# A 128-byte padding tile ahead of the probability, weight, K and V tiles of a cached GQA attention block

## The chip, the cores and the metric

The kernel runs on one core of a Trainium2 chip. The metric is the device time of one execution in microseconds. Before the change the median of 12 runs is 192.56 us (192.39 to 192.72).

## The reference

A block of grouped-query attention for decoding: 8 sequences with 4 new tokens each, 32 query heads on 8 key/value heads, a cache of 2048 positions, head size 128, all in bfloat16.

```python
q = (x @ wq).reshape(B, Sq, Hq, Dh).transpose(0, 2, 1, 3)      # x: (8, 4, 512), wq: (512, 4096)
k = repeat(k_cache, 4, axis=1)                                  # k_cache, v_cache: (8, 8, 2048, 128)
v = repeat(v_cache, 4, axis=1)
p = softmax(q @ k^T * 128 ** -0.5)
return (p @ v).transpose(0, 2, 1, 3).reshape(B, Sq, 4096) @ wo  # wo: (4096, 512)
```

K and V are 33.6 MB each, wq and wo 4.2 MB each: some 75.5 MB are read once, and little else moves.

## The kernel before

**Units.** The work is cut into 32 units `(p, b)`: a pair `p` of key/value heads of one sequence `b`. A unit's K is one tile `k_sb` of 128 partitions by 32 x 128 elements (8 KB in each partition, 1 MB in all); partition `s` holds 32 neighbouring cache positions, so each partition is filled from one unbroken run of 8 KB in HBM. V is laid out in the same way in `v_sb`. `kpool` has 7 buffers and `vpool` has 6.

**Loads.** All loads are issued by SyncE (SP), in the order of the list `loads` that is made at L113 to L121: `wq` (L111, 32 KB in each partition) and `x` (L112) first, then K three units ahead of V in turn, and the pieces of `wo` (L109) behind the last of them. `load_ready` (L123) issues what has a free buffer; it is called once in each half-unit step. `wo_sb` takes over the place of `wq_sb` in SBUF (L189; the pool `wpool` has one buffer). `wo` comes in two pieces of 8 KB in each partition, three of 4 KB and two of 2 KB.

**Steps.** The loop at L317 goes over half units. Each step transposes half of a K tile on TensorE through PSUM (L199; two bf16 values travel as one fp32), copies the result to `kt` (L206 on VectorE, a quarter of them at L204 on ScalarE), forms the scores of the half before (L217) and their exponentials into `probs` (L227), sums the probabilities with a matrix of ones (L255, L263, L267), multiplies them with V (L241) and scales (L272). After each head pair the result is transposed (L284, L299), and at the end it is multiplied with `wo` (L309), evacuated (L361, L362) and stored (L363, L364). The order on each engine is the order of the code (`manual_schedule`, L65).

**Placement in SBUF.** The pools are laid out one behind the other in the order of L53 to L58, and the tiles of `const` in the order in which the code names them. An address below is the byte at which a tile starts in each partition. `const` begins with `x_sb` at 16,512, which is 32 x 512 + 128; with the sizes of the tiles that follow, `xT_sb` (256 bytes) being the first that is no multiple of 512, `qT_all` and all that come behind it up to `ident` start 384 bytes past a multiple of 512, `ones` 128 bytes past one, and `probs` again 384. Since `probs`, `wq_sb`/`wo_sb`, `k_sb`, `v_sb` and `kt` are whole multiples of 512 bytes, each of their buffers starts 384 bytes past a multiple of 512, that is, 128 past a multiple of 256: `wq_sb` and `wo_sb` at 44,928, the first `k_sb` at 77,696, the first `v_sb` at 135,040, the first `kt` at 184,192.

Of the kernel before, what the change touches and what calls it, by code (L numbers as in the profile page):

```python
# [8 lines left out]
BF16 = mybir.dt.bfloat16  # L9
# [5 lines left out]
def kernel(  # L15
# [37 lines left out]
    const = ctx.enter_context(tc.tile_pool(name="const", bufs=1))  # L53
# [24 lines left out]
    oP = [const.tile([128, WR, T], BF16, name=f"oP{p}") for p in range(G2)]  # L78
    ident = const.tile([128, 128], BF16, name="ident")
    ones = const.tile([128, 128], BF16, name="ones")  # L80
    probs = [const.tile([128, C, NQ], BF16, name=f"probs{i}") for i in range(L // 2 + 2)]

    units = [(p, b) for p in range(G2) for b in range(B)]
# [311 lines left out]
```

The softmax here doesn't subtract the row's maximum and nothing guards it: scores larger than these inputs give would overflow.

## Time and profile before

| | |
|---|---|
| median of 12 runs | 192.56 us (192.39 to 192.72) |
| the profiled execution, time of the run | 192.41 us |
| its span, first to last instruction | 190.6 us |
| granted TensorE clock | 1.0 |
| busy: PE, PE weight load, VectorE, ScalarE | 152.7, 139.5, 113.8, 86.2 us |
| read from HBM | 75.53 MB, 396 GB/s over the span |
| K and V load: size, median from issue to landing | 1024 KB, 19.9 us |
| longest wait of TensorE for DMA within the loop | 10.8 us in all, for K (L199) |

The span leaves out what lies ahead of the first instruction and behind the last: 1.8 us of the run. Busy times of different engines overlap, so they don't add up to the span. TensorE is busy for 80% of it, but the row of the DMA engines (shown below) is the one that is full from the start to the last load.

### The profile page before, as it was taken

What the parts mean: (1) busy time and instruction counts of PE and PEld (TensorE: products, weight loads), DVE (VectorE), ACT (ScalarE), POOL (GpSimd) and SP (SyncE); (2) the same over time, 40 slices, a digit from 0 to 9 for tenths busy, and PEclk for the clock granted to TensorE, in tenths of its full rate; (3) what the DMA queues carried; (4) which work ended last, traced back from release to release, by engine and by line L of the source; (5) the groups of instructions that cost most, each with busy time, mean ns of one, the idle gap of its engine ahead of it and who ended that gap; (6) DMA issues with size and microseconds to landing.
All of it is one profiled execution on the core that took longest, in us unless ns stands there. A gap on an engine that the chain in (4) does not pass through costs nothing.

```text
span 190.6 us, 6429 instructions
## 1 busy us (share of the span) xinstructions
PE 152.7 (80%) x2861; PEld 139.5 (73%) x2892; DVE 113.8 (60%) x220; ACT 86.2 (45%) x170; POOL 1.1 (1%) x8
## 2 busy tenths in 40 slices
PE   0019887899999999978888889998885899998683
PEld 0018776799989998867888878887774788886572
DVE  6411745577767777666666667776663677672420
ACT  2003466665566654555544444454553555551000
POOL 2000000000000000000000000000000000000000
PEclk9999999999999999999999999999999999999999
DMA  6999999999999999999999999999999999999950
GB/s 227 433 407 421 419 425 411 425 419 421 418 414 416 428 411 416 425 418 419 421 416 423 418 416 423 414 418 423 418 421 416 418 428 413 416 424 414 413 206 9
DMA packets 10539, 75.97 MB, mean 399 GB/s; under 512 B 1200, under 2 KB 1296, under 8 KB 1936
## 3 DMA queue, kind: packets, MB, share of 16 engines
q1 hardware_dynamic: 10464, 75.55, 95.8%
q8 instruction: 22, 0.36, 0.8%
q14 instruction: 5, 0.04, 0.1%
q10 hardware_dynamic: 48, 0.02, 0.0%
HBM read 75.53 MB, written 0.03 MB: 396 GB/s over the span
## 4 chain that ended last, share of the span: by engine, by line
DMA 90%; PE 7%; DVE 1%; ACT 0%; issue 0%; SPq 0%
DMA k_sb<-in_k_cache_dram 74%; DMA wo_sb<-in_wo_dram 9%; DMA x_sb<-in_x_dram 6%; PE psq L161 2%; PE out_ps L309 2%; PE kp L199 2%; DVE q_bd L185 1%; PE pse L176 1%; ACT q_bd L185 0%; PE xtp L152 0%; PE s_ps L217 0%; SPq L111 0%; ACT out_sb L362 0%; DVE xT_sb L155 0%
## 5 line engine op out<-in xcount | busy, mean ns | idle before, releaser
L199 PE MATMUL kp<-ident,k_sb 128*128 128x128 f32 x512 | 80.9, 284 | 10.8 <-DMA k_sb<-in_k_cache_dram 10.8
L206 DVE COPY kt<-kp 128x1024 bf16<-128x1024 bf16 x96 | 65.5, 685 | 27.0 <-PE kp L199 26.4
L227 ACT ACTIVATE probs<-s_ps 64x256 bf16<-64x256 f32 x128 | 48.3, 378 | 69.0 <-PE s_ps L217 68.2
L199 PEld LDWEIGHTS kp<-ident,k_sb 128*128 128x128 f32 x512 | 55.2, 143 | 12.2 <-issue 11.8
L217 PE MATMUL s_ps<-q_bd,kt 128*128 128x64 bf16 x1024 | 42.1, 193 | 3.1 <-ACT kt L204 2.6
L217 PEld LDWEIGHTS <-kt 128*128 128x128 bf16 x1024 | 39.6, 98 | 4.8 <-ACT kt L204 3.1
L241 PEld LDWEIGHTS <-v_sb 128*128 128x128 bf16 x1024 | 34.2, 96 | 9.7 <-DMA v_sb<-in_v_cache_dram 2.5
L263 DVE TENSOR_REDUCE l_sb<-l_ps 128x32 f32<-128x512 f32 x32 | 22.1, 692 | 24.0 <-PE l_ps L255 21.2
L241 PE MATMUL o_ps<-probs,v_sb 128*128 128x32 bf16 x1024 | 35.0, 176 | 1.3 <-DMA v_sb<-in_v_cache_dram 1.2
L204 ACT COPY kt<-kp 128x1024 bf16<-128x1024 bf16 x32 | 32.4, 1012 | 0.8
L255 PE MATMUL l_ps<-probs,ones 128*128 128x512 bf16 x33 | 12.4, 380 | 1.5
L267 DVE RECIPROCAL r_sb<-l_sb 128x32 f32<-128x32 f32 x32 | 11.3, 353 | 1.1
L152 PE MATMUL xtp<-ident,x_sb 32*128 32x32 bf16 x4 | 0.5, 190 | 13.5 <-DMA x_sb<-in_x_dram 13.3
L152 PEld LDWEIGHTS <-x_sb 32*128 32x128 bf16 x4 | 0.3, 115 | 13.6 <-DMA x_sb<-in_x_dram 13.3
L309 PE MATMUL out_ps<-wo_sb,oP 128*32 128x256 bf16 x64 | 7.6, 272 | 1.3 <-DMA wo_sb<-in_wo_dram 1.3
L168 ACT ACTIVATE qT_all<-psq 128x256 bf16<-128x256 f32 x4 | 1.5, 383 | 14.6 <-PE psq L161 14.6
L309 PEld LDWEIGHTS <-oP 128*32 128x32 bf16 x64 | 6.1, 96 | 2.0 <-issue 1.2
L362 ACT CAST out_sb<-out_ps 32x256 bf16<-32x256 f32 x1 | 0.4, 361 | 15.1 <-PE out_ps L309 15.1
L272 DVE TENSOR_TENSOR oT_all<-o_ps,r_sb 128x32 bf16<-128x32 f32 x32 | 5.8, 182 | 1.7 <-PE o_ps L241 1.5
L255 PEld LDWEIGHTS <-ones 128*128 128x128 bf16 x64 | 6.0, 98 | 0.8 <-issue 0.4
L185 DVE CAST q_bd<-pse 64x512 bf16<-64x512 f32 x4 | 2.6, 683 | 4.7 <-PE pse L176 4.7
L155 DVE COPY xT_sb<-xtp 128x32 bf16<-128x32 bf16 x4 | 0.5, 170 | 6.8 <-PE xtp L152 6.8
(23 smaller groups left out, 34.4 us busy)
## 6 DMA issues: line engine op xcount, KB each, us to landing
k_sb<-in_k_cache_dram SPq DMA_DIRECT2D x32, 1024.0 KB, 19.9
v_sb<-in_v_cache_dram SPq DMA_DIRECT2D x32, 1024.0 KB, 19.9
wq_sb<-in_wq_dram SPq DMA_DIRECT2D x1, 4096.0 KB, 12.3
wo_sb<-in_wo_dram SPq DMA_DIRECT2D x2, 1024.0 KB, 18.7
wo_sb<-in_wo_dram SPq DMA_DIRECT2D x3, 512.0 KB, 17.5
wo_sb<-in_wo_dram SPq DMA_DIRECT2D x2, 256.0 KB, 13.4
x_sb<-in_x_dram SPq DMA_DIRECT2D x1, 32.0 KB, 12.1
out_dram<-out_sb SPq DMA_DIRECT2D x1, 16.0 KB, 1.4
```

The costliest lines, as they stand in the source:

```text
L185: (nc.scalar.copy if g else nc.vector.tensor_copy)(out=q_bd[rows, p, :, :, g, :], in_=pse[rows, :, :, :])
L199: nc.tensor.transpose(kp[:, j, :], k4[:, w : w + 128], ident4[:, :])
L204: nc.scalar.copy(out=kt2, in_=kp2)
L206: nc.vector.tensor_copy(out=kt2, in_=kp2)
L217: nc.tensor.matmul(s_ps[:, 2 * j : 2 * j + 2, :], lhsT=k_t[:, j % (HC // 4), :, e], rhs=q_bd[:, p, e, b, :, :], start=(e == 0), stop=(e == 1),
L227: nc.scalar.activation(out=pr[rows, hf * HC : (hf + 1) * HC, cols], in_=s_ps[rows, :, cols], func=EXP)
L241: nc.tensor.matmul(o_ps[u][:, :], lhsT=vs[u][:, cc, :], rhs=pr[:, cc, :], start=(cc == 0), stop=(cc == C - 1),)
L255: nc.tensor.matmul(l_ps[:, :, :], lhsT=ones[:, :], rhs=pr[:, c : c + LC, :], start=(c == 0), stop=(c + LC == C),)
L263: nc.vector.tensor_reduce(out=l_sb[:, :], in_=l_ps[:, :, :].rearrange("d c q -> d q c"), axis=AX, op=ADD)
L267: nc.vector.reciprocal(r_sb[:, :], l_sb[:, :])
L272: nc.vector.tensor_tensor(out=oT_all[:, p * HP : (p + 1) * HP, b, :], in0=o_ps[u][:, :].rearrange("d (h s) -> d h s", h=HP), in1=r_sbs[u][ ...
L309: nc.tensor.matmul(out_ps[half][:, :], lhsT=oP[p][:, r, :], rhs=wo_sb[:, p, r, half * DH : (half + 1) * DH], start=(p == 0 and r == 0), st ...
```

## The change

One tile more is named in the pool `const`, between `ones` and `probs`. Nothing reads or writes it.

```diff
     ident = const.tile([128, 128], BF16, name="ident")
     ones = const.tile([128, 128], BF16, name="ones")
+    pad = const.tile([128, 64], BF16, name="pad")
     probs = [const.tile([128, C, NQ], BF16, name=f"probs{i}") for i in range(L // 2 + 2)]
```

The tile takes 64 bf16 elements, 128 bytes, in each partition. All that lies behind it moves up by 128 bytes; all ahead of it stays.

| tile | start before | start after | after, past a multiple of 512 |
|---|---|---|---|
| `x_sb` | 16,512 | 16,512 | 128 |
| `q_bd` | 19,840 | 19,840 | 384 |
| `ident4`, `oT_all`, `out_sb`, `oP`, `ident` | | unmoved | 384 |
| `ones` | 34,432 | 34,432 | 128 |
| `probs0` (five of 2,048 bytes) | 34,688 | 34,816 | 0 |
| `wq_sb`, `wo_sb` | 44,928 | 45,056 | 0 |
| `k_sb`, first of 7 (8,192 bytes each) | 77,696 | 77,824 | 0 |
| `v_sb`, first of 6 (8,192 bytes each) | 135,040 | 135,168 | 0 |
| `kt`, first of 6 (2,048 bytes each) | 184,192 | 184,320 | 0 |
| `l_sb` (two of 128 bytes) | 196,480 | 196,608 | 0 and 128 |
| `r_sb` (two of 128 bytes) | 196,736 | 196,864 | 256 and 384 |
| `nat_sb`, first of 2 | 196,992 | 197,120 | 0 |

PSUM is laid out as before. The instructions of every engine, their order and their waits are the same in both programs; only the addresses in SBUF differ.

## The prediction, as it was written before the changed kernel ran

> **What bounds the kernel now.** I read the page's DMA rows first, then the chain that ended last, then the waits of SP's queue, then the busy times by stretch. In the DMA rows each digit is the busy share of the 16 DMA engines in one fortieth of the span (9 is 90% or more), GB/s is what they moved, and q1 is the queue that carries all of SP's loads.
>
> ```profile
> DMA  6999999999999999999999999999999999999950
> GB/s 227 433 407 421 419 425 411 425 419 421 418 414 416 428 411 416 425 418 419 421 416 423 418 416 423 414 418 423 418 421 416 418 428 413 416 424 414 413 206 9
> DMA packets 10539, 75.97 MB, mean 399 GB/s; under 512 B 1200, under 2 KB 1296, under 8 KB 1936
> ...
> q1 hardware_dynamic: 10464, 75.55, 95.8%
> ```
>
> The engines are full from the second slice to the last load. Only the length of each packet, or the number of bytes, can shorten that. The chain in order of time (start, duration, what) says the same.
>
> ```profile
> 1.17 12.05 DMA x_sb<-in_x_dram
> ...
> 20.80 2.56 PE kp L199 x12
> 23.36 0.50 PE s_ps L217 x16
> 23.85 0.63 PE kp L199 x6
> 24.48 19.80 DMA k_sb<-in_k_cache_dram
> ...
> 166.48 17.48 DMA wo_sb<-in_wo_dram
> ...
> 184.00 3.67 PE out_ps L309 x32
> ```
>
> From 24.48 to 184.00 us it is loads only. Each step is one load from issue to landing; it takes 19.80 us because seven others are queued ahead of it: 8 x 1.0486 MB in 19.80 us is 423.7 GB/s. The waits of SP's queue (total us, times, longest) show what lets the next load go.
>
> ```profile
> SPq L102 <- DMA v_sb<-in_v_cache_dram: 56.0, 25, 3.6
> SPq L92 <- DMA k_sb<-in_k_cache_dram: 50.7, 25, 2.1
> ...
> SPq L102 <- PE o_ps L241: 4.4, 4, 2.2
> ```
>
> Nearly always it is an earlier landing. TensorE held a load back a few times, for 2.2 us at most, while some 7 loads of about 2.5 us each were still queued: the stream doesn't run dry.
>
> **The change.** It removes no instruction, adds none, moves none on any engine and adds no wait. It shifts SBUF addresses by 128 bytes: loads of wq, wo, K and V write from a multiple of 512 instead of 384 past one; TensorE, VectorE and ScalarE meet probs, kt and V at other addresses.
>
> *DMA packets, the one item on the path.* How many: 64 K and V loads of 128 rows are 8192 packets of 8 KB; wo is 256 of 8 KB, 384 of 4 KB, 256 of 2 KB; wq is 128 of 32 KB. That is 9216, or 576 for each of the 16 engines. (The rest of q1 are 4-byte completions and the few rows of x and out, which stay where they were.)
>
> How long one takes: q1's 95.8% of 16 x 190.6 us is 2921.5 us of packet time. The trace's packet records give the commonest duration by size: 1 KB 46 ns, 2 KB 84, 4 KB 159, 8 KB 309, 32 KB 1213. The slope from 4 to 32 KB is (1213 - 159) / 28,672 = 0.03676 ns a byte, 27.2 GB/s for an engine; what is left is 8.4 ns for each packet (159 - 150.6), the same for 1 KB and for 32 KB. The mean 8 KB packet is 314.6 ns, 5.5 over its commonest: jitter.
>
> So 8.4 ns a packet and the jitter are all that an address could touch. Bounds: nothing (the 8.4 ns belong to any packet), or all of the 8.4 ns: 576 x 8.4 = 4.8 us. With the jitter gone too it would be 576 x 13.9 = 8.0 us, and I see no reason for that. Below nothing: see the last rival.
>
> [...] And every large packet of this trace with an SBUF end starts 128 past a multiple of 256, x and out included, so no row shows an aligned one. [...]
>
> *Where the 2.7 us land.* Head: x lands at 13.22 us behind wq's 8 packets per engine, 0.04 us sooner. From there to 24.48 us TensorE's chain rules, but seven loads stay queued, so the engines don't stop and the stream gains all the while. End: the last V lands near 180.3 us, with about 560 of the 576 packets of each engine behind it, so 2.6 us sooner; the last wo pieces gain the rest. Behind 184.00 us 3.67 us of L309, the evacuation and the store of 16 KB stand as they were.
>
> *Is TensorE able to follow?* Columns: the stretch, its length, then busy us (count) of PE, weight load, VectorE, ScalarE, POOL, the granted clock, DMA share and GB/s.
>
> ```profile
> 44.00:64.00 20.00, 19.74 (x394) 18.58 (x396) 14.79 (x29) 12.61 (x25) 0.00 (x0) 1.00 1.01 418
> ...
> 84.00:105.00 21.00, 17.14 (x341) 15.83 (x343) 13.46 (x25) 10.86 (x22) 0.00 (x0) 1.00 1.02 421
> ...
> 145.00:166.00 21.00, 17.48 (x337) 16.40 (x342) 13.07 (x26) 9.37 (x21) 0.00 (x0) 1.00 1.01 419
> ```
>
> At 44 to 64 us it is full, catching up from its late start on a stock of loaded tiles; from 84 us on it idles 17 to 18%, waiting for K. The stream gets 1.4% quicker (2.7 of 184 us), so cover remains. If it were gone, the gain would end where TensorE is full: 20 us at 1.4%, 0.3 us given up.
>
> *Operands at new addresses.* L217 (193 ns), L241 (176), L206 (685), L227 (378), L255 (380): no row shows any of them at another address. Bounds: plus or minus a few per cent. PE's 152.7 us lie within 13.3 to 187.7 us, with 21.7 us idle, so a slowdown is hidden until its 2861 matmuls lose some 7 ns each, 4% of L241's duration; a speed-up is worth nothing but a little of the 3.67 us at the end. I take zero.
>
> **Sum.** Against the profiled run: 192.41 - 2.7 = 189.7. That run lies 0.15 under the median, so 192.56 - 2.7 = 189.9 us.
>
> **Rivals.**
> *No effect, 192.6 us.* The 8.4 ns are the packet's own. [...] Chance 0.24.
> [...] Chance 0.12, within "faster".
> *Slower, 195.7 us.* Rows that now all start on the same 512-byte grid meet more often, and the jitter doubles: 5.5 ns x 576 = 3.2 us. For it: mean and commonest packet do differ, so something already collides, and the stream has no slack at all; it decides from 0.7 ns a packet (0.2% of 309). Against it: all buffers already start at one common offset, and their spacing is unchanged. Chance 0.17, most of it for a loss smaller than this.
>
> **Numbers.** 0.2%, 0.4 us, is about what a measurement of this kernel can tell from no change. Forecast (4 cycles, or a gain of that order between 0.4 and 4 us) 0.47; full transaction 0.12; no effect 0.24; slower 0.17. So faster 0.59, same 0.24, slower 0.17. The likeliest alone runs from 188.6 to 192.1. For eight in ten I go from 187.4, near the full transaction, to 192.9, which takes in no effect and a trace of loss.
>
> **What would show it.** Right: the commonest 8 KB packet near 304 to 305 ns, 4 KB near 154, q1's share of packet time down by 2.7 us per engine, slices near 426 GB/s, chain steps of a K load near 19.5 us instead of 19.80, x still at 46 ns and the completions at 9. Matmul durations the same. Wrong: the same packet times with the time unchanged (no effect), a wider gap between mean and commonest packet (the last rival), or quicker packets with SP's queue now waiting for L241 and L199 (TensorE became the bound).

## The result and the profile after

The changed kernel takes 190.18 us (median of 7 runs, 190.07 to 190.37) against 192.57 us for the kernel before (29 runs): the ratio is 0.9878, with a 95% interval of 0.9869 to 0.9887, or 2.4 us. Its profiled execution took 190.18 us with a span of 188.4 us, 2.2 us under the span before. Two of the five executions of dma_on_grid, its profiled one among them, and one of the four of pieces_on_grid took over 1.5% longer than the fastest of their kernel and are left out of the times below.

The DMA rows of the page after:

```profile
DMA  6999999999999999999999999999999999999950
GB/s 223 445 397 426 421 433 417 426 428 421 421 426 421 430 419 423 428 424 419 431 421 421 431 421 423 428 421 426 424 421 430 419 430 423 424 422 418 421 218 9
...
q1 hardware_dynamic: 10464, 75.55, 95.7%
```

There are as many packets and bytes on q1 as before, and the engines are as full as before. But 95.7% of a span of 188.4 us is 180.3 us for each engine, where 95.8% of 190.6 was 182.6 us. So 2.3 us of packet time are gone from each engine, and they are the whole gain.

The chain of waits of the kernel after, in order of time:

```profile
24.31 19.47 DMA k_sb<-in_k_cache_dram
43.80 19.80 DMA k_sb<-in_k_cache_dram
63.62 20.90 DMA k_sb<-in_k_cache_dram
84.53 19.49 DMA k_sb<-in_k_cache_dram
...
144.81 19.50 DMA k_sb<-in_k_cache_dram
164.33 17.42 DMA wo_sb<-in_wo_dram
...
181.80 3.67 PE out_ps L310 x32
```

Of the chain before, the steps behind the first (24.48, 19.80):

```profile
44.30 19.90 DMA k_sb<-in_k_cache_dram
64.22 21.33 DMA k_sb<-in_k_cache_dram
85.57 19.83 DMA k_sb<-in_k_cache_dram
```

The loads still make the chain. The first step is 19.47 us instead of 19.80, the first three together 60.17 instead of 61.03; the last load is through at 181.75 us (164.33 + 17.42), where it was 183.96; the 3.67 us of products behind it are what they were (all lines of the code have moved down by one: L310 is the former L309).

Did TensorE become a bound? First the waits of SP's queue after the change, then the busy times by stretch:

```profile
SPq L103 <- DMA v_sb<-in_v_cache_dram: 55.5, 25, 3.5
SPq L93 <- DMA k_sb<-in_k_cache_dram: 51.2, 26, 2.2
...
SPq L103 <- PE o_ps L242: 2.6, 3, 1.6
```

```profile
44.00:64.00 20.00, 19.79 (x405) 18.82 (x407) 15.35 (x30) 12.08 (x24) 0.00 (x0) 1.00 1.01 423
...
84.00:105.00 21.00, 17.42 (x341) 16.24 (x346) 13.33 (x26) 10.19 (x21) 0.00 (x0) 1.00 1.01 426
...
145.00:166.00 21.00, 20.00 (x361) 18.86 (x366) 13.87 (x27) 10.09 (x20) 0.00 (x0) 0.92 1.01 424
```

It did not: the loads are let go by landings, TensorE holds them back for 2.6 us where it was 4.4, and its share of 84 to 105 us has risen only from 17.14 to 17.42 us. From 145 to 166 us it has risen from 17.48 to 20.00 us, in an execution whose granted clock was 0.92 there instead of 1.00; the chain's step in that stretch (19.50 us) is no longer than the others, so that cost nothing, but little idle time was left. The operands at new addresses cost what they cost before, as the groups of the page after show (busy us, mean ns; before 685, 378, 193 and 176 ns):

```profile
L207 DVE COPY kt<-kp 128x1024 bf16<-128x1024 bf16 x96 | 65.2, 683 | 26.2 <-PE kp L200 25.7
L228 ACT ACTIVATE probs<-s_ps 64x256 bf16<-64x256 f32 x128 | 48.3, 378 | 67.6 <-PE s_ps L218 66.9
...
L218 PE MATMUL s_ps<-q_bd,kt 128*128 128x64 bf16 x1024 | 42.8, 194 | 3.4 <-ACT kt L205 2.6
...
L242 PE MATMUL o_ps<-probs,v_sb 128*128 128x32 bf16 x1024 | 35.1, 177 | 1.0 <-DMA v_sb<-in_v_cache_dram 0.9
```

**What changed within a packet.** The packet records of q1 in the two traces:

| packets of q1 | before: commonest, share of it, mean | after: commonest, share of it, mean |
|---|---|---|
| 8 KB, 8448 | 309 ns, 37%, 314.5 | 309 ns, 99.6%, 310.5 |
| 4 KB, 384 | 159 ns, 62%, 161.0 | 159 ns, 100%, 159.0 |
| 2 KB, 256 | 84 ns, 93%, 84.2 | 84 ns, 100%, 84.0 |
| 32 KB (wq), 128 | 1213 ns, 66%, 1304.8 | 1213 ns, 63%, 1301.7 |
| 4 bytes (completions), 1184 | 9 ns, 84%, 9.5 | 9 ns, 99.7%, 9.0 |

Between these two kernels the commonest duration has not moved for any size. What is gone is the scatter above it. For an engine that is 528 packets of 8 KB by 3.95 ns (2.09 us), 24 of 4 KB by 2.0 (0.05), 74 completions by 0.5 (0.04) and 8 of 32 KB by 3.1 (0.03), in all 2.2 us: the difference of the two spans.

### The profile page after: what moved, and what is told of

Same layout as the page of the kernel before. It is cut to its first block, busy times and chain, and to the rows that moved or that the text cites. A ratio compares the mean times of both kernels' runs of the same rounds, so it can differ in the third digit from the quotient of the medians.

```text
span 188.4 us, 6429 instructions
## 1 busy us (share of the span) xinstructions
PE 152.5 (81%) x2861; PEld 139.3 (74%) x2892; DVE 113.3 (60%) x220; ACT 86.2 (46%) x170; POOL 1.1 (1%) x8
## 3 DMA queue, kind: packets, MB, share of 16 engines
q1 hardware_dynamic: 10464, 75.55, 95.7%
## 4 chain that ended last, share of the span: by engine, by line
DMA 95%; PE 2%; SPq 1%; issue 0%; ACT 0%
DMA k_sb<-in_k_cache_dram 85%; DMA wo_sb<-in_wo_dram 9%; PE out_ps L310 2%; SPq L93 1%; SPq L113 0%; SPq L112 0%; ACT out_sb L363 0%
## 5 line engine op out<-in xcount | busy, mean ns | idle before, releaser
L218 PE MATMUL s_ps<-q_bd,kt 128*128 128x64 bf16 x1024 | 42.8, 194 | 3.4 <-ACT kt L205 2.6
L310 PE MATMUL out_ps<-wo_sb,oP 128*32 128x256 bf16 x64 | 7.6, 272 | 1.0 <-DMA wo_sb<-in_wo_dram 1.0
L310 PEld LDWEIGHTS <-oP 128*32 128x32 bf16 x64 | 6.1, 96 | 1.8 <-issue 1.0
L363 ACT CAST out_sb<-out_ps 32x256 bf16<-32x256 f32 x1 | 0.4, 361 | 14.5 <-PE out_ps L310 14.5
```

Source lines behind the costliest of these rows:

```text
L218: nc.tensor.matmul(s_ps[:, 2 * j : 2 * j + 2, :], lhsT=k_t[:, j % (HC // 4), :, e], rhs=q_bd[:, p, e, b, :, :], start=(e == 0), stop=(e == 1),
L310: nc.tensor.matmul(out_ps[half][:, :], lhsT=oP[p][:, r, :], rhs=wo_sb[:, p, r, half * DH : (half + 1) * DH], start=(p == 0 and r == 0), st ...
```

## The experiments

The question left by these tables is whose scatter it was: that of the written addresses or of the compute engines' operands, of one border or another, of the DMA engines alone or of their meeting with the compute engines. The theories go by letters: A, a write off the border is drawn out where it meets the compute engines in SBUF; B, by itself; C, it is the place of the operands of the compute engines that counts; D and E, two prices that the author set for B (D, the same for any start off the border, at either end and for a packet of any size; E, one that grows with the distance from the border below); F, it is the difference between the read and the written end.

### Which tiles, and which border

Two kernels put only one kind of tile on the border, by gaps of chosen sizes between the pools; three more change the size of the pad.

```diff
 # dma_on_grid: 128 bytes ahead of wpool, 384 bytes ahead of ktpool
+    gap1 = ctx.enter_context(tc.tile_pool(name="gap1", bufs=1))
     wpool = ctx.enter_context(tc.tile_pool(name="wpool", bufs=1))
...
+    gap2 = ctx.enter_context(tc.tile_pool(name="gap2", bufs=1))
     ktpool = ctx.enter_context(tc.tile_pool(name="ktpool", bufs=6))
...
+    gap1.tile([128, 64], BF16, name="pad1")
+    gap2.tile([128, 192], BF16, name="pad2")
```

> Only wq, wo, K and V, the tiles that DMAs write, start on multiples of 512 bytes; probs, kt and the small tiles start 384 past one, as before. Theory A and B (the written end of the DMA packets matters): the whole gain is here, 190.2 us within 0.4, nearly all 8 KB packets at 309 ns. Theory C (what matters is where the tiles lie that TensorE, VectorE and ScalarE read and write in the loop): 192.6 us, two in three packets above 309 ns, mean near 314.6.

```diff
 # engines_on_grid: 128 bytes ahead of probs, 384 ahead of wpool, 128 ahead of ktpool
+    pad = const.tile([128, 64], BF16, name="pad")
...
+    gap1.tile([128, 192], BF16, name="pad1")
+    gap2.tile([128, 64], BF16, name="pad2")
```

> The reverse: probs, kt and the small tiles as in the changed kernel, on multiples of 512; wq, wo, K and V start 384 past one, as before. Theory A and B: 192.6 us within 0.4, mean 8 KB packet near 314.6 ns. Theory C: 190.2 us, packets at 309 ns.

```diff
 # pad_to_256, pad_to_64 and pad_to_32: only the size of the pad
-    pad = const.tile([128, 64], BF16, name="pad")
+    pad = const.tile([128, 192], BF16, name="pad")   # pad_to_256
+    pad = const.tile([128, 32], BF16, name="pad")    # pad_to_64
+    pad = const.tile([128, 80], BF16, name="pad")    # pad_to_32
```

> The pad takes 384 bytes in each partition instead of 128: the same tiles start 256 past a multiple of 512. If the border that matters is one of 256 bytes, as the prediction had it: 190.2 us, packets at 309 ns. If it is one of 512: 192.6 us, packets as before.

> The pad takes 64 bytes: the same tiles start 448 past a multiple of 512, 64 short of a border. If the cost comes with any start off the border: 192.6 us, commonest packet 309 ns and mean near 314.6 as before. If only a start of 128 past one is dear (or if 64 bytes are the grid): 190.2 us. If the distance decides (192 bytes past a 256-byte border instead of 128): between 193 and 195 us.

> The pad takes 160 bytes: the tiles start 32 past a multiple of 512. [...]

Measured, with the packet records of each one's profile (mean of those under 360 ns, which leaves out the few longer ones that come with instruction fetches, 27 in the kernel before):

| kernel | K, V, wq, wo past a 256-byte border | probs, kt past it | us, median | ratio to before, 95% | 8 KB packets at 309 ns, mean in ns |
|---|---|---|---|---|---|
| before | 128 | 128 | 192.57 | | 37%, 312.9 |
| changed | 0 | 0 | 190.18 | 0.9869 to 0.9887 | 99.6%, 309.0 |
| dma_on_grid | 0 | 128 | 190.24 | 0.987 to 0.991 | 99.5%, 309.0 (from 60 us on) |
| engines_on_grid | 128 | 0 | 192.57 | 0.9993 to 1.0011 | 36%, 312.9 |
| pad_to_256 | 0 (256 past one of 512) | 0 | 190.15 | 0.9862 to 0.9891 | 99.5%, 309.0 |
| pad_to_64 | 192 | 192 | 192.80 | 1.0005 to 1.0024 | 8%, 313.7 (commonest 312) |
| pad_to_32 | 32 | 32 | 193.26 | 1.0021 to 1.0044 | 8%, 314.5 (commonest 313) |

The profile of dma_on_grid (span 191.6 us) shows 1,451 packets of 330 to 360 ns, nearly all in its first 50 us, where the other six of the table show none; they have no explanation here, and behind them its packets are those of the changed kernel. The chain of waits of engines_on_grid, then that of pad_to_256:

```profile
24.71 19.80 DMA k_sb<-in_k_cache_dram
44.53 19.82 DMA k_sb<-in_k_cache_dram
64.36 21.37 DMA k_sb<-in_k_cache_dram
```

```profile
24.08 19.70 DMA k_sb<-in_k_cache_dram
43.79 19.70 DMA k_sb<-in_k_cache_dram
63.51 20.77 DMA k_sb<-in_k_cache_dram
```

Three steps are 60.99 us in the first and 60.17 in the second; in the changed kernel they are 60.17 too.

What follows. The gain lies with the tiles that DMAs write: dma_on_grid's interval takes in the whole of it. Where probs and kt lie is worth nothing (theory C falls). The border is one of 256 bytes, not of 512: pad_to_256, 256 past a multiple of 512, took 190.15 us. And the loss does not grow with the distance from the border: 32 bytes past it is the worst of the three (193.26 us, against 192.57 at 128 and 192.80 at 192). Theory E falls with that. Theory D had the three off-border kernels equal; pad_to_32 and pad_to_64 are 0.6 and 0.3 us over the runs of the kernel before that were timed with each, so it is near but not exact. In these two the commonest packet has moved as well, to 313 and 312 ns, which neither the expectation of pad_to_64 (309) nor a price by distance has: 32 bytes past the border raised it by 4 ns, 192 by 3, and 128, in the kernel before, by nothing.

### The DMA engines alone, or their meeting with the compute engines

A quiet kernel keeps all loads in their order and drops nearly all of the work in the loop.

```diff
 # quiet_off_grid (quiet_on_grid: the same with the pad of 128 bytes)
-            transpose_part(i, 0)
+            touch_k(i)            # one transpose of 128 x 128
...
-            scores(j)
...
-            values(step)
+            touch_v(step)         # one product with one piece of V
```

> The kernel before with nearly all work in the loop left out, so the output is not the attention: each half step only transposes one 128 x 128 piece of K and multiplies one piece of V, to let the buffers go; the loads, their order and their addresses (384 past a multiple of 512) are as before, and VectorE and ScalarE are silent in the loop. Theory A (a write that starts off the border is drawn out when the compute engines use SBUF beside it): 8 KB packets at 309 ns nearly all, the same time as the quiet kernel on the border within 0.4 us. Theory B (a write off the border is drawn out by itself): mean near 314.6 ns, two in three above 309, and 2.4 us more than the quiet kernel on the border.

> The same quiet kernel, with the same work left out, and the pad of 128 bytes of the changed kernel. Both theories: 8 KB packets at 309 ns nearly all; some 188 to 190 us, since loads end where they do in the changed kernel and little is left behind them.

> The kernel before, off the border, with TensorE's work in the loop whole and that of VectorE and ScalarE left out (no copies of K, no exponentials, no sums; TensorE reads tiles that were zeroed once, so the output is not the attention). Theory A with TensorE's reads of SBUF as the partner: 8 KB packets drawn out as before, mean near 314.6 ns. Theory A with the writes of VectorE and ScalarE as the partner: 309 ns nearly all. Theory B: near 314.6.

> The quiet kernel off the border, and beside its loads VectorE copies 210 and ScalarE 142 times from one fixed PSUM tile to the kt tiles in SBUF, without a pause until some 165 us (work of the loop left out as in the quiet kernel). Theory A with the writes of VectorE and ScalarE as the partner: drawn out at least as before, mean 314 ns or more. Theory A with TensorE as the partner: 309 ns nearly all. Theory B: near 314.6.

Measured: 191.86 us (190.24 to 192.51) off the border and 188.92 us (188.53 to 190.00) on it. That is 2.9 us where theory B had 2.4, but single times of one kernel lie up to 2.3 us apart, so the chain is the finer measure. The chain of waits of the quiet kernel off the border, then of the one on it:

```profile
44.38 19.87 DMA k_sb<-in_k_cache_dram
64.27 19.89 DMA k_sb<-in_k_cache_dram
84.17 19.88 DMA k_sb<-in_k_cache_dram
...
163.71 17.46 DMA wo_sb<-in_wo_dram
```

```profile
43.70 19.61 DMA k_sb<-in_k_cache_dram
63.33 19.61 DMA k_sb<-in_k_cache_dram
82.95 19.61 DMA k_sb<-in_k_cache_dram
...
161.46 17.20 DMA wo_sb<-in_wo_dram
```

Each step of eight loads takes 0.27 us more off the border, or 4.2 ns for each of the 64 packets of an engine, and the last load is through 2.5 us later (181.17 us, on the border 178.66). How quiet it was shows in its busy times from 44 to 64 us (off the border; the zeros are VectorE, ScalarE and POOL):

```profile
44.00:64.00 20.00, 4.01 (x16) 2.18 (x16) 0.00 (x0) 0.00 (x0) 0.00 (x0) 0.50 1.01 421
```

The 8 KB packets, all of them taken: 27% at 309 ns and a mean of 313.8 off the border, 99.9% and 309.2 on it; the kernel before has 37% and 314.5. With TensorE alone at full work (tensor_only_off, 149.8 us busy) the mean is 314.3, 35% at 309 (194.28 us in a single run, with other work left out than in the quiet kernels). In vector_scalar_off ScalarE's copies came behind VectorE's and after the loads, which the expectation did not have, as the slices show:

```profile
DVE  7039999999999999999990000000000000000000
ACT  1040000000000000000009999999999999999996
...
DMA  7999999999999999999999999900000000000000
```

So it tests VectorE alone, at full work through most of the loads: 313.8 ns. (Its 281.85 us are that tail of ScalarE.) Theory A falls, and theory B stands: a write off the border is drawn out by itself, with VectorE and ScalarE silent and TensorE nearly so, or with them busy.

### The read end, and the size of the packets

source_off_grid reads K and V of the quiet kernel from 128 bytes further on in HBM, so that both ends of a packet are off by the same amount if the two tensors begin on a 256-byte border, which no run shows; the shift moves the read end by half of 256 bytes in any case (only the last pair of heads is left unshifted). The other pair cuts each load in four.

```diff
 # source_off_grid, in load_k and load_v
+        at = min((b * Hkv + 2 * p) * Sk * Dh + 64, (B * Hkv - 2) * Sk * Dh)
...
-            k_cache[b, 2 * p : 2 * p + 2].rearrange("g (s c) d -> (g s) c d", c=C),
+            k_cache.rearrange("b h s d -> (b h s d)")[at : at + 128 * C * Dh].rearrange(
+                "(q c d) -> q c d", c=C, d=Dh
+            ),
 # pieces_off_grid (pieces_on_grid: with the pad), in load_k and load_v
-        nc.sync.dma_start(ks[u][:, :, :], ...)
+        for c0 in range(0, C, C // 4):
+            nc.sync.dma_start(ks[u][:, c0 : c0 + C // 4, :], rows[:, c0 : c0 + C // 4, :])
```

> The quiet kernel (most work of the loop left out, and K and V read from 128 bytes further on in HBM, so the output is not the attention), with the tiles 384 past a multiple of 512 as before: source and destination are now off the 256-byte border by the same amount. Theory F (what counts is that a packet's two ends lie differently to the border): 8 KB packets at one value nearly all, 309 to 314 ns, and about 188.9 us. [...]

> The kernel before, off the border, with each K and V load issued as four DMAs of 2 KB in each partition: 2048 packets of 2 KB per engine instead of 512 of 8 KB. [...] If the surplus goes with the bytes: 2.4 us more, as with whole loads. [...]

> The same with the pad of 128 bytes. Both: 2 KB packets at 84 ns nearly all; 14.4 us more than the changed kernel (1536 more packets per engine at 8.4 ns, 192 more completions at 9 ns), so near 204.6 us, if the queue stays full with eight loads of 256 KB in flight.

source_off_grid took 192.97 us in a single run; the steps of the chain are a finer measure than that. Its chain of waits in the same stretch as the quiet kernels:

```profile
44.60 19.86 DMA k_sb<-in_k_cache_dram
64.48 19.86 DMA k_sb<-in_k_cache_dram
84.36 19.86 DMA k_sb<-in_k_cache_dram
```

The steps are those of the quiet kernel off the border (19.87 to 19.89; one later step, of 20.26 us, stands out), the mean packet is 313.8 ns in both, and the commonest is still 309. So theory D falls at the read end, and theory F is out as well: the shift of the source by 128 bytes adds nothing and heals nothing. Of the two ends it is the written one that counts here.

The cut loads: 216.80 us (215.14 to 217.71) off the border, 212.51 us (210.62 to 213.56) on it, both far over the 204.6 us that the packets' count gave for the latter. The transfer rates and the row of q1, first off, then on the border:

```profile
GB/s 281 409 299 384 391 379 363 332 330 361 336 393 342 330 346 391 379 384 330 360 374 330 378 392 381 376 369 384 337 363 325 364 391 368 378 363 390 406 364 14
...
q1 hardware_dynamic: 38112, 75.56, 97.7%
```

```profile
GB/s 283 421 287 403 406 397 379 376 347 307 378 371 347 355 380 398 396 400 343 393 352 385 361 370 351 394 374 339 396 399 386 369 393 390 387 360 393 418 365 16
...
q1 hardware_dynamic: 38112, 75.56, 98.4%
```

Slices go down to 307 GB/s, and yet the packets fill nearly the whole span: it is the packets that are longer. Of the 33,024 packets of 2 KB, 1,127 off the border and 1,009 on it took more than 100 ns; over 84 ns each, these add up to 11.9 and 10.0 us for an engine. What draws them out when loads are cut into pieces of 256 KB is not shown.

Among the packets under 100 ns the mean is 85.1 ns off and 84.0 on the border. These 1.1 ns make some 2.2 us for an engine, about what was expected of a loss that goes with the bytes (2.4 us), and not what theory D would have: at the 3.95 ns that an 8 KB packet lost, 2048 packets of any size would lose 8.1 us, by estimate. With the 2.0 ns of a 4 KB and the 3.9 ns of an 8 KB packet in the kernel before it makes a row in which the loss grows with the bytes; the last 256 packets of 2 KB of that kernel (0.2 ns) and those of wq don't fit into it. The times differ by 4.3 us; the rest lies in the long packets and in pauses, and is not assigned to the border here.

## Why the prediction came out right

*The bound, and that the gain passes on whole.* Right. The 2.2 us that packets lost per engine are the 2.2 us that the span lost. TensorE was able to follow, the operands' durations did not move, and x was used 0.09 us sooner (first transpose at 13.18 us, before 13.27) where 0.04 was worked out.

*The size.* 2.7 us were predicted for the run, 2.4 measured (192.57 - 190.18). The 2.7 us of the sum are 4.7 ns for each of 576 packets, a term that no run shows; what the runs showed in its place is 3.95 ns for an 8 KB packet (314.48 to 310.53 ns) and less for the small ones. A gain of the whole 8.4 ns a packet (4.8 us), to which the forecast gave 0.12, is out, and so are the slower rival and no effect.

*The step that failed* is the price itself: no row of the trace before shows that 4.7 of the 8.4 ns over a packet's bytes go with the border. The prediction's sign for it, commonest packets near 304 and 154 ns, did not come: they stayed at 309 and 159 with the tiles on the border. So the 8.4 ns stand over a packet's bytes on the border too; the 4-byte completions, commonly 9 ns before and after, fit with that. Nor does a price by distance show elsewhere: in pad_to_32 a start 32 bytes past the border cost more than one 128 past it (193.26 against 192.57 us), and in source_off_grid a source moved by 128 bytes left the commonest packet at 309 ns.

*What took its place* is the term that the prediction set aside: the scatter of 5.5 ns above the commonest packet, for which it saw "no reason" to go. Of its 5.5 ns (the mean before is 314.5 ns, not 314.6) 3.95 went; what is left is 1.5 ns, from 27 packets of 549 to 855 ns. The trace before has 27 over 360 ns as well. In both traces the queues that fetch instructions (q8 and q14) carry 27 packets from 10 us on, and each drawn-out packet starts within 1.1 us of the start of one of these: the pad does not touch that part of the scatter. The last rival had the same term with the sign turned round. That two different terms of nearly one size were at hand, 4.7 and 3.95 ns, is luck, and it made a right number out of a wrong reason.

*What stays open.* Why a write off a 256-byte border is drawn out. In every kernel off the border the packets of wq show it no more than those on the border (79 to 84 of 128 at 1213 ns off it, 81 to 85 on it), and the first load of K is nearly clean until about 14.5 us (in the kernel before all 115 packets of 8 KB until then took 309 ns); from 16 us on most packets show it. No run here isolates a cause of that, and theory D's one price does not hold by distance, by packet or at the read end. The size by distance (3.9 ns at 128 bytes past the border, 4.7 at 192, 5.5 at 32, taken over 309.0 from the means without the packets over 360 ns) has no explanation either.

## What to carry to other kernels

Where a kernel is bound by its loads, look at where its load tiles start in SBUF: a start off a multiple of 256 bytes cost 1.3% here (192.57 against 190.18 us; 1.6% at 32 bytes past it, 193.26 us), and 128 bytes of padding, which no instruction touches, gave it back. Align the tiles that DMAs write; moving those that only the compute engines use by 128 bytes changed nothing here, and a multiple of 512 brought no more than one of 256. When the durations of DMA packets are read, look at the commonest value and at the scatter above it, each by itself: at 128 bytes past the border only the scatter could be removed, at 32 and at 192 bytes the commonest value had moved too (313 and 312 ns), and a trace of one address alone doesn't tell which part belongs to the address.

## What the runs showed of the hardware that was not expected

- A DMA's written address and its read address count differently: 128 bytes off at the written end lengthened 8 KB packets by 3.9 ns on average, the same shift at the read end by nothing (313.8 ns with and without).
- The completions, packets of 4 bytes, lost their scatter too (84% at 9 ns before, 99.7% after). Their scatter does not simply follow that of the data packets: at 32 bytes past the border, where these were drawn out most, 99.5% of the completions took 9 ns.
- The chain's longer steps (21.3 us before, 20.9 after, one in three) are absent in the quiet kernels, where all are alike to 0.1 us; these fetch 2 instruction packets on q8 instead of 22. The drawn-out data packets go with the fetches one by one (3 with 3 in the quiet kernels, counting q8 and q14, and 27 with 27 in the kernel before and the changed one), so that the fetches make the longer steps is likely; it was not tried alone.
- The same light work of TensorE ran at two granted clocks. From 44 to 64 us it was busy for 20% of the time in quiet_off_grid and in source_off_grid, and the clock was 0.50 in the one and 1.00 in the other; two of the ten executions of quiet_off_grid had a mean of 0.98, the others 0.58. The steps of the loads are alike at both clocks (19.87 to 19.89 and 19.86 us). The clock by slices, first of quiet_off_grid, then of source_off_grid (tenths, 9 is 90% or more):

```profile
PEclk9999855555555555555555555555555555555858
```

```profile
PEclk9999999999999999999999999999999999999958
```
